# Running products in place of logarithm and exponential in a state-space scan with a cosine-gated FFN

## The chip, the cores and the metric

The kernel runs on one core of a Trainium2 chip. The metric is device time in microseconds (us). A kernel's time is the median of several runs; each run also records the length of its instruction span and the mean clock that the throttle granted to TensorE. TensorE does the matmuls (PE in the profile, PEld for its weight loads), DVE is VectorE, ACT is ScalarE, POOL is GpSimd, SP issues the DMAs.

## The reference, cut to what matters

For 4 batches, 8 heads and 768 positions, a decaying state of 16 x 32 is carried along the sequence; then an FFN with `h * cos(h)` follows.

```python
cum = np.cumsum(np.log(np.clip(a, 1e-06, 1.0)), axis=-1)         # in a chunk
L = np.exp(cum[..., :, None] - cum[..., None, :]) * causal       # decay from j to i
y = ((C @ B.T) * L) @ x + (C @ state) * np.exp(cum)[..., None]
state = np.exp(total) * state + sum_j(B_j x_j * exp(total - cum_j))
...
h = y @ w_in;  g = h * np.cos(h);  out = g @ w_out
```

The kernel works in six chunks of 128 positions. A decay between two positions is a product of `a`, so it can come from sums of logarithms or from a running product.

## The kernel before

One FFN **step** takes 128 of the 2048 inner columns for all four batches of a chunk: `first(n)` makes `h`, `gate(n-1)` the cosine and the product, `second(n-3)` the output sum. There are 96 steps, 16 a chunk. During the steps of chunk c the scan of chunk c+1 is done, one batch in three steps: decays and transposes (`turn`), then `intra`, then `finish` with the state update (`carry`). In the steps of chunk 0 the weights are also rounded, piece by piece: `grade` (ACT, POOL), then `join` (DVE twice, then an integer add on POOL).

```python
# the start: decays of whole chunks from sums of logarithms
ACT.activation(la, la, AF.Ln)
def whole():
    for u in range(NU):
        PE.transpose(lt_ps[:, u], la[:, u], ident[0:RB, 0:RB])
    ACT.copy(out=laT, in_=...)
    for i, tri in enumerate((upto, after, ones)):
        PE.matmul(d_ps, lhsT=tri, rhs=laT, start=True, stop=True)
        ACT.activation(dec[:, i], d_ps, AF.Exp)
    ACT.activation(..., quarter, AF.Sin)              # loads the sine's table
...
# in the loop
V.tensor_tensor_scan(out=l, data0=arow, data1=unit, initial=0.0, op0=mult, op1=add)   # lam
G.tensor_tensor(out=sc[:, i], in0=src, in1=dec[:, d, c] ..., op=ALU.mult)   # C and B scaled
PE.transpose(tp[:, 2], sc[:, 0, heads(b)] ..., ident)                       # scaled C
...
V.tensor_tensor(out=new, in0=s_ps, in1=own, op=ALU.mult)                    # carry
G.tensor_tensor(out=old, in0=state.pop((c - 1, b)), in1=dec[:, 2, c, ...], op=ALU.mult)
G.tensor_tensor(out=new, in0=new, in1=old, op=ALU.add)
...
for n in range(NC * NF + LAG):
    first(n)                                    # PE, then ACT k, DVE w
    if c == 0: grade(*order[n + 3])             # ACT mag and last, POOL clamp
    gate(n - 1)                                 # ACT sine, DVE gT
    second(n - LAG)
    if c == 0: join(*order[n + 2])              # DVE, DVE, POOL add
    # carry, then decays and turn, intra or finish of one batch of chunk c + 1
```

Of the kernel before, what the change touches and what calls it, by code (L numbers as in the profile page):

```python
# [8 lines left out]
FP32 = mybir.dt.float32  # L9
U32 = mybir.dt.uint32  # L10
I32 = mybir.dt.int32
AF = mybir.ActivationFunctionType
ALU = mybir.AluOpType
# [12 lines left out]
def kernel(  # L26
# [22 lines left out]
    nc = tc.nc  # L49
    V, ACT, G, PE = nc.vector, nc.scalar, nc.gpsimd, nc.tensor  # L50

    NB, H, S, D = x.shape
    N = B.shape[-1]
    P = 128
# [25 lines left out]
    def bank(shape, name, tag="scan"):  # L80
        return psum.tile(shape, FP32, tag=tag, bufs=BANKS[tag], name=name)


    raw, arow = {}, {}
    ones = const.tile([P, P], FP32, name="ones")
    V.memset(ones, 1.0)

    def fill(dst, times=1):

        for _ in range(times):  # L90
            PE.matmul(dst, lhsT=ones, rhs=ones.unsqueeze(1).to_broadcast([P, dst.shape[1], P]),  # L91
                      start=True, stop=True, skip_group_check=True)


    a_cut = dram.tile([NB, H, S], FP32, name="a_cut")

    def load(c, each=False):
# [13 lines left out]
    def load_a(c, seqs=range(NB)):  # L111
        if c >= NC:
            return
        for b in seqs:
            arow[c, b] = t = rows.tile([P, H, P], FP32, tag="arow", name="arow")
            nc.sync.dma_start(
                out=t, in_=a_cut[b, :, c * P:(c + 1) * P].unsqueeze(0).to_broadcast([P, H, P]))

    a_in = const.tile([RB, NU, P], FP32, name="a_in")
    nc.sync.dma_start(  # L120
# [60 lines left out]
    for n in range(6):  # L181
# [5 lines left out]
    quarter = const.tile([P, 1], FP32, name="quarter")  # L187
    V.memset(quarter, HALF_PI)

    upto = const.tile([P, P], FP32, name="upto")  # L190
    G.affine_select(out=upto, in_=ones, pattern=[[1, P]], compare_op=ALU.is_ge, fill=0.0,
                    base=0, channel_multiplier=-1)
    after = const.tile([P, P], FP32, name="after")
    G.affine_select(out=after, in_=ones, pattern=[[-1, P]], compare_op=ALU.is_gt, fill=0.0,
                    base=0, channel_multiplier=1)

    unit = const.tile([P, H, P], FP32, name="unit")
    V.tensor_copy(out=unit, in_=ident.unsqueeze(1).to_broadcast([P, H, P]))

# [8 lines left out]
    V.tensor_tensor(out=slot, in0=own[:, 0:HH, 0], in1=own[:, HH:H, 0], op=ALU.add)  # L208


    la = const.tile([RB, NU, P], FP32, name="la")
    V.tensor_scalar(out=la, in0=a_in, scalar1=1e-6, scalar2=1.0, op0=ALU.max, op1=ALU.min)
    cut = const.tile([RB, NU, P], FP32, name="cut")
    G.tensor_scalar(out=cut, in0=a_in, scalar1=1.0, scalar2=1e-6, op0=ALU.min, op1=ALU.max)
    G.memset(cut[:, :, 0:1], 0.0)
    nc.sync.dma_start(out=a_cut.rearrange("(u b) h (c p) -> (b h c) u p", u=NU, p=P), in_=cut)
    ACT.activation(la, la, AF.Ln)
    dec = const.tile([P, 3, NC, NB * H], FP32, name="dec")

    def whole():  # L220

        lt_ps = bank([P, NU, RB], "lt_ps")
        for u in range(NU):
            PE.transpose(lt_ps[:, u], la[:, u], ident[0:RB, 0:RB])
        laT = const.tile([P, NB * H * NC], FP32, name="laT")
        ACT.copy(out=laT, in_=lt_ps.rearrange("p u r -> p (u r)"))
        for i, tri in enumerate((upto, after, ones)):
            d_ps = bank([P, NB * H, NC], "d_ps")
            PE.matmul(d_ps.rearrange("p r c -> p (r c)"), lhsT=tri, rhs=laT,
                      start=True, stop=True)  # L230
            ACT.activation(dec[:, i].rearrange("p c r -> p r c"), d_ps, AF.Exp)

        ACT.activation(const.tile([P, 1], FP32, name="sine"), quarter, AF.Sin)


    scaled, lam, state, part, yT = {}, {}, {}, {}, {}

    def prep(c):

        if c >= NC:  # L240
            return
        bc = raw[c][0]
        scaled[c] = sc = scan.tile([P, 2, NB * H, N], FP32, tag="sc", name="sc")
        for i, (src, d) in enumerate(((bc[:, 1], 0), (bc[:, 0], 1))):
            if i == 0 and c == 0:
                continue
            G.tensor_tensor(
                out=sc[:, i], in0=src,
                in1=dec[:, d, c].unsqueeze(2).to_broadcast([P, NB * H, N]), op=ALU.mult)

    def heads(b):
        return slice(b * H, (b + 1) * H)
# [14 lines left out]

    def decays(c, b):

        lam[c, b] = l = scan.tile([P, H, P], FP32, tag="lam", bufs=3, name="lam")  # L270
        if c > 0:
            V.tensor_tensor_scan(  # L272
                out=l.rearrange("p h i -> p (h i)"),
                data0=arow.pop((c, b)).rearrange("p h i -> p (h i)"),
                data1=unit.rearrange("p h i -> p (h i)"), initial=0.0,
                op0=ALU.mult, op1=ALU.add)
            return
        for t, a_ps in enumerate(spread.pop(b)):
            V.tensor_tensor_scan(
                out=l[:, t * HH:(t + 1) * HH].rearrange("p h i -> p (h i)"),  # L280
                data0=a_ps.rearrange("p h i -> p (h i)"),
                data1=unit[:, 0:HH].rearrange("p h i -> p (h i)"), initial=0.0,
                op0=ALU.mult, op1=ALU.add)

    def turn(c, b):
        bc, sc = raw[c][0], scaled.get(c)
        tp = bank([P, 3, P], "tp")
        PE.transpose(tp[:, 0], bc[:, 0, heads(b)].rearrange("p h n -> p (h n)"), ident)
        PE.transpose(tp[:, 1], bc[:, 1, heads(b)].rearrange("p h n -> p (h n)"), ident)
        if c > 0:  # L290
            PE.transpose(tp[:, 2], sc[:, 0, heads(b)].rearrange("p h n -> p (h n)"), ident)  # L291

        cT = scan.tile([P, HH, P], FP32, tag="cT", name="cT")
        for t in range(HH):
            ACT.activation(cT[:, t], tp[:, 1], AF.Copy, scale=slot[:, t:t + 1])  # L295
        bcT = scan.tile([P, 2, P], FP32, tag="bcT", name="bcT")
        if c > 0:
            ACT.copy(out=bcT, in_=tp[:, 0:3:2])
        else:
            ACT.copy(out=bcT[:, 0], in_=tp[:, 0])  # L300
        part[c, b] = (bcT, cT)

    def intra(c, b):
# [36 lines left out]
    def carry(c, b):  # L340
        if c == NC - 1:
            return
        xr, sc = raw[c][1], scaled[c]
        s_ps = bank([P, H, D], "s_ps")
        PE.matmul(s_ps.rearrange("p h d -> p (h d)"),  # L345
                  lhsT=sc[:, 1, heads(b)].rearrange("p h n -> p (h n)"),
                  rhs=xr[:, b].rearrange("p h d -> p (h d)"), start=True, stop=True)
        state[c, b] = new = states.tile([P, H, D], FP32, tag="state", name="state")
        V.tensor_tensor(out=new, in0=s_ps, in1=own, op=ALU.mult)  # L349
        if c > 0:  # L350
            old = scan.tile([P, H, D], FP32, tag="old", name="old")
            G.tensor_tensor(
                out=old, in0=state.pop((c - 1, b)),
                in1=dec[:, 2, c, heads(b)].unsqueeze(2).to_broadcast([P, H, D]), op=ALU.mult)
            G.tensor_tensor(out=new, in0=new, in1=old, op=ALU.add)  # L355


    hp, turns, gT, o = {}, {}, {}, {}
# [39 lines left out]


    tags = (("h", "h"), ("h", "o"), ("h", "h"), ("h", "o"))  # L400
    fill(bank([P, 1, P], "warm", "o"), 8)
    spread_a(0, tags[0])
    whole()
    spread_a(1, tags[1])
    decays(0, 0)
    turn(0, 0)
    decays(0, 1)
    turn(0, 1)
    prep(0)
    intra(0, 0)  # L410
    spread_a(2, tags[2])
    decays(0, 2)
    intra(0, 1)
    finish(0, 0)
    spread_a(3, tags[3])
    decays(0, 3)
    turn(0, 2)
    turn(0, 3)
    finish(0, 1, 1)
    grade(*order[0])  # L420
    intra(0, 2)
    join(*order[0])
    intra(0, 3)
    finish(0, 2, 2)
    finish(0, 3, 2)
    grade(*order[1])
    grade(*order[2])
    join(*order[1])
    join(*order[2])
    load(1)  # L430
    for b in range(NB):
        load_a(1, (b,))
        for n in (6 + 2 * b, 7 + 2 * b):
            fetch(*order[n])
# [4 lines left out]
    for n in range(NC * NF + LAG):  # L439
        c, f = divmod(n, NF)  # L440
        if n < NC * NF:
            if f == 0 and c > 0:
                load(c + 2)
            first(n)
        if c == 0 and n + 3 < len(order):
            grade(*order[n + 3])
        if 0 <= n - 1 < NC * NF:
            gate(n - 1)
        if n >= LAG:
            second(n - LAG)  # L450
        if c == 0 and n + 2 < len(order):
            join(*order[n + 2])
        if n < NB:
            carry(0, n)
        if n == 1:
            prep(1)
        if c + 1 < NC:
            b, j = divmod(f - 3, 3)
            if 0 <= b < NB:
                if j == 0:  # L460
                    decays(c + 1, b)
                (turn, intra, finish)[j](c + 1, b)
            if f == NF - 1:
                raw.pop(c + 1)
                load_a(c + 2)
                prep(c + 2)


# [28 lines left out]
```

## Time and profile before

| | first trace | second trace, taken later |
|---|---|---|
| time of that run, us | 437.95 | 435.16 |
| span, us | 436.2 | 433.4 |
| mean granted clock | 0.992 | 0.996 |
| step 0 starts | 30.34 | 27.63 |
| step 6 starts | 55.33 | 52.53 |
| step 16 starts | 101.58 | 98.78 |
| step 16 to the end | 334.6 | 334.6 |

The median was 435.42 us. The second trace is of the usual kind. Here are its stretches of 2 us around the place where the first trace's clock was 0.50. Columns: stretch, length, busy time and count of PE, PEld, DVE, ACT and POOL, then granted clock, DMA share and GB/s.

```profile
12.00:14.00 2.00, 1.65 (x9) 0.90 (x10) 0.49 (x1) 1.49 (x7) 0.68 (x1) 1.00 1.02 324
14.00:16.00 2.00, 2.00 (x18) 1.57 (x16) 2.00 (x4) 0.00 (x0) 0.00 (x0) 1.00 1.05 392
```

The clock stays at 1.00. Nearly all that differs between the two traces lies before step 0 (from there to step 16 they take 71.2 us each). The times show the two kinds too: of the 48 runs of the kernel before that were taken for comparison, 36 lie between 434.85 and 435.65 us and 12 between 437.95 and 438.05 us, with nothing between.

### The profile page before, as it was taken

How to read it: one execution, taken by the hardware profiler on the slowest of the kernel's cores; microseconds unless marked ns; L12 is line 12 of the kernel's file. 1: busy time of each engine (PE TensorE's matmuls, PEld its weight loads, DVE VectorE, ACT ScalarE, POOL GpSimd, SP SyncE). 2: the span in 40 equal slices, each digit the busy share in tenths (PEclk: the TensorE clock that was granted, in tenths of full speed). 3: DMA queues.
4: the chain of work that ended last, by engine and by line, in shares of the span. 5: the costliest groups of instructions: out<-in, count | busy, mean ns of one | idle time of the engine just before them, and what ended most of it. 6: DMA issues, size and time to landing. Idle time of an engine off the chain costs nothing.

```text
span 436.2 us, 5099 instructions
## 1 busy us (share of the span) xinstructions
PE 424.1 (97%) x1918; PEld 274.8 (63%) x1918; DVE 241.6 (55%) x332; ACT 184.8 (42%) x383; POOL 72.5 (17%) x87
## 2 busy tenths in 40 slices
PE   8898999999999999999999999999999999999996
PEld 8544656656666656666566665666656666666665
DVE  4657976873654653546553465554465545344332
ACT  4366656543532433534442444433344433343332
POOL 2027664753011013010113001112000000000000
PEclk9898999999999999999999999999999999999999
DMA  7999698156211147111119021001010000010001
GB/s 92 315 131 345 213 136 139 48 80 66 67 31 48 50 71 75 50 48 48 50 32 114 27 70 50 29 20 50 0 50 0 0 2 0 2 48 0 0 2 48
DMA packets 103017, 28.84 MB, mean 66 GB/s; under 512 B 74960, under 2 KB 98896, under 8 KB 102992
## 3 DMA queue, kind: packets, MB, share of 16 engines
q1 hardware_dynamic: 102992, 28.51, 32.3%
q8 instruction: 15, 0.25, 0.2%
q14 instruction: 10, 0.08, 0.1%
HBM read 25.26 MB, written 3.24 MB: 65 GB/s over the span
## 4 chain that ended last, share of the span: by engine, by line
PE 91%; ACT 3%; POOL 2%; DVE 1%; issue 1%; ACTq 0%; POOLq 0%
PE hp L364 37%; PE o L385 36%; PE g L310 5%; PE y L331 3%; PE s_ps L345 2%; POOL w_in L176 2%; PE y L327 2%; PE a_ps L264 2%; PE warm L91 1%; ACT mag L156 1%; ACT cT L295 1%; DVE mag L172 1%; DVE mag L170 1%; ACT last L158 1%; PE y L91 0%
## 5 line engine op out<-in xcount | busy, mean ns | idle before, releaser
L364 PE MATMUL hp<-yT,w_in 128*128 128x512 f32 x384 | 184.6, 603 | 4.8 <-POOL w_in L176 4.2
L385 PEld LDWEIGHTS o<-w_out,gT 128*128 128x128 f32 x768 | 146.1, 190 | 59.3 <-issue 44.4
L385 PE MATMUL o<-w_out,gT 128*128 128x256 f32 x768 | 181.0, 379 | 0.0
L370 DVE SCALAR_TENSOR_TENSOR w<-hp,k 128x512 f32<-128x512 f32 x96 | 66.2, 690 | 135.1 <-ACT k L368 135.1
L368 ACT ACTIVATE k<-hp 128x512 int32<-128x512 f32 x96 | 57.3, 597 | 185.0 <-PE hp L364 184.6
L364 PEld LDWEIGHTS hp<-yT,w_in 128*128 128x128 f32 x384 | 69.8, 191 | 70.6 <-issue 48.5
L377 DVE TENSOR_TENSOR gT<-hp,w 128x512 f32<-128x512 f32 x96 | 66.3, 691 | 5.9 <-ACT w L375 5.7
L375 ACT ACTIVATE w<-w,quarter 128x512 f32<-128x512 f32 x96 | 68.5, 713 | 0.1
L272 DVE TENSOR_TENSOR_SCAN lam<-arow,unit 128x1024 f32<-128x1024 f32 x20 | 46.6, 2329 | 0.0
L355 POOL TENSOR_TENSOR state<-state,old 128x256 f32<-128x256 f32 x16 | 11.6, 725 | 185.2 <-DVE state L349 185.0
L313 DVE TENSOR_TENSOR m<-g,lam 128x512 f32<-128x512 f32 x48 | 30.9, 684 | 16.5 <-PE g L310 16.5
L295 ACT ACTIVATE cT<-tp,slot 128x128 f32<-128x128 f32 x96 | 27.4, 371 | 14.3 <-PE tp L291 12.4
L310 PE MATMUL g<-cT,bcT 64*128 64x512 f32 x96 | 28.5, 656 | 2.0 <-ACT bcT L300 1.9
L336 ACT COPY yT<-y 128x256 f32<-128x256 f32 x24 | 9.0, 376 | 35.5 <-PE y L331 35.5
L349 DVE TENSOR_TENSOR state<-s_ps,own 128x256 f32<-128x256 f32 x20 | 8.4, 422 | 18.6 <-PE s_ps L345 18.6
L176 POOL TENSOR_TENSOR w_in<-mag,last 128x512 uint32<-128x512 uint32 x8 | 14.0, 1751 | 12.8 <-DVE mag L172 12.8
L331 PE MATMUL y<-m,xr 128*32 128x128 f32 x384 | 15.5, 279 | 0.0
L159 POOL TENSOR_SCALAR mag<-mag 128x512 f32<-128x512 f32 x16 | 11.8, 738 | 16.1 <-ACT mag L156 16.1
L310 PEld LDWEIGHTS g<-cT,bcT 64*128 64x128 f32 x96 | 7.5, 185 | 10.5 <-ACT w L375 5.6
L345 PE MATMUL s_ps<-xr,sc 128*128 128x256 f32 x40 | 14.0, 434 | 0.0
L176 POOL TENSOR_TENSOR w_out<-mag,last 128x512 uint32<-128x512 uint32 x8 | 12.1, 1506 | 10.3 <-DVE mag L172 10.3
L327 PEld LDWEIGHTS y<-bcT,state 128*128 128x128 f32 x80 | 12.1, 191 | 1.0
(59 smaller groups left out, 190.4 us busy)
## 6 DMA issues: line engine op xcount, KB each, us to landing
arow<-a_cut SPq DMA_DIRECT2D x20, 512.0 KB, 4.0
words<-in_moe_w_in_dram SPq DMA_DIRECT2D x8, 512.0 KB, 6.5
words<-in_moe_w_out_dram SPq DMA_DIRECT2D x8, 512.0 KB, 7.0
out_dram<-ob SPq DMA_DIRECT2D x12, 256.0 KB, 2.2
xr<-in_x_dram SPq DMA_DIRECT2D x5, 512.0 KB, 8.8
bc<-in_B_dram SPq DMA_DIRECT2D x5, 256.0 KB, 7.3
bc<-in_C_dram SPq DMA_DIRECT2D x5, 256.0 KB, 9.4
xr<-in_x_dram SPq DMA_DIRECT2D x4, 128.0 KB, 3.7
```

The source lines that it names most:

```text
L176: G.tensor_tensor(out=dst.bitcast(U32), in0=bits.rearrange("p (k f) -> p k f", k=k), in1=last.rearrange("p (k f) -> p k f", k=k), op=ALU.add)
L272: V.tensor_tensor_scan(out=l.rearrange("p h i -> p (h i)"), data0=arow.pop((c, b)).rearrange("p h i -> p (h i)"), data1=unit.rearrange("p ...
L295: ACT.activation(cT[:, t], tp[:, 1], AF.Copy, scale=slot[:, t:t + 1])
L310: PE.matmul(g[u], lhsT=bcT[r, 0], rhs=cT[r], start=True, stop=True)
L313: V.tensor_tensor(out=m[:, hs], in0=g[u], in1=l[:, hs], op=ALU.mult)
L331: PE.matmul(y[32 * q:32 * q + 32, t], lhsT=xr[:, b, h], rhs=m[:, h], start=(c == 0 and t == 0), stop=True, tile_position=(0, 32 * q), skip ...
L364: PE.matmul(hp[n], lhsT=w_in[:, k, f * P:(f + 1) * P], rhs=yT[c][:, k], start=(k == 0), stop=(k == KT - 1))
L368: ACT.activation(k, hp[n], AF.Copy, bias=0.25, scale=INV_2PI)
L370: V.scalar_tensor_tensor(out=w, in0=hp[n], scalar=INV_2PI, in1=k, op0=ALU.mult, op1=ALU.subtract)
L375: ACT.activation(cos, cos, AF.Sin, bias=quarter, scale=TWO_PI)
L377: V.tensor_tensor(out=gT[n], in0=hp.pop(n), in1=cos, op=ALU.mult)
L385: PE.matmul(o[c][b // 2][:, b % 2], lhsT=g[:, b * P:(b + 1) * P], rhs=w_out[:, f], start=(f == 0 and b % 2 == 0), stop=(f == NF - 1), skip ...
```

## The change

Its intent: no logarithm, no exponential and no change of activation table; one transpose less per batch and chunk; the state update in one operation. The decay up to i becomes a second running product (`reach`) over rows of `a` that a DMA spreads over the partitions, and C is scaled as it is copied out of its transpose. B's decay is the last column of the scan that is there anyway.

```diff
-    ACT.activation(la, la, AF.Ln)
-    def whole(): ...                              # sums, Exp, tables
+    def load_along(c):                            # 4 new DMAs a chunk, 64 KB each
+        for b in range(NB):
+            nc.sync.dma_start(out=t[:, b], in_=a_all[b, :, c * P:(c + 1) * P] ...)
...
     (in decays)
+            V.tensor_tensor_scan(out=r, data0=along[c][:, b], data1=ones, initial=1.0,
+                                 op0=ALU.mult, op1=ALU.mult)               # reach
+        G.tensor_tensor(out=sc, in0=raw[c][0][:, 0, heads(b)],
+                        in1=lam[c, b][:, :, P - 1:P] ..., op=ALU.mult)      # B scaled
     (in turn)
-            PE.transpose(tp[:, 2], sc[:, 0, heads(b)] ..., ident)
+            V.tensor_tensor(out=bcT[:, 1], in0=tp[:, 1], in1=reach[c, b], op=ALU.mult)
     (in carry)
-            G.tensor_tensor(out=old, ...)
-            G.tensor_tensor(out=new, in0=new, in1=old, op=ALU.add)
+            V.scalar_tensor_tensor(out=new, in0=state.pop((c - 1, b)),
+                                   scalar=reach[c, b][:, P - 1:P], in1=new, op0=mult, op1=add)
     (the start)
-    fill(bank([P, 1, P], "warm", "o"), 8)
+    fill(bank([P, 1, P], "warm", "o"), 6)
     ...
+    grade(*order[1]); grade(*order[2])            # these moved ahead of finish(0, 3)
     finish(0, 3, 2)
+    join(*order[2]); join(*order[1])              # was 1, then 2
     load(1)
+    load_along(1)                                 # ahead of the weight pieces from 6 on
```

More of the change, by code (lines that the diff above doesn't have):

```diff
@@ L81, in bank @@
         return psum.tile(shape, FP32, tag=tag, bufs=BANKS[tag], name=name)
-    raw, arow = {}, {}
+    raw, arow, along = {}, {}, {}
     ones = const.tile([P, P], FP32, name="ones")
@@ L92, in fill @@
                       start=True, stop=True, skip_group_check=True)
+    a_all = dram.tile([NB, H, S], FP32, name="a_all")
     a_cut = dram.tile([NB, H, S], FP32, name="a_cut")
@@ L117, in load_a @@
                 out=t, in_=a_cut[b, :, c * P:(c + 1) * P].unsqueeze(0).to_broadcast([P, H, P]))
+    def load_along(c):
+        if c >= NC:
+            return
+        along[c] = t = rows.tile([P, NB, P], FP32, tag="along", bufs=2, name="along")
+        for b in range(NB):
+            nc.sync.dma_start(
+                out=t[:, b], in_=a_all[b, :, c * P:(c + 1) * P].unsqueeze(1)
+                .to_broadcast([H, N, P]))
     a_in = const.tile([RB, NU, P], FP32, name="a_in")
@@ L188 @@
     V.memset(quarter, HALF_PI)
-    upto = const.tile([P, P], FP32, name="upto")
-    G.affine_select(out=upto, in_=ones, pattern=[[1, P]], compare_op=ALU.is_ge, fill=0.0,
-                    base=0, channel_multiplier=-1)
-    after = const.tile([P, P], FP32, name="after")
-    G.affine_select(out=after, in_=ones, pattern=[[-1, P]], compare_op=ALU.is_gt, fill=0.0,
-                    base=0, channel_multiplier=1)
     unit = const.tile([P, H, P], FP32, name="unit")
@@ L208 @@
     V.tensor_tensor(out=slot, in0=own[:, 0:HH, 0], in1=own[:, HH:H, 0], op=ALU.add)
-    la = const.tile([RB, NU, P], FP32, name="la")
-    V.tensor_scalar(out=la, in0=a_in, scalar1=1e-6, scalar2=1.0, op0=ALU.max, op1=ALU.min)
     cut = const.tile([RB, NU, P], FP32, name="cut")
@@ L215 @@
     G.memset(cut[:, :, 0:1], 0.0)
-    nc.sync.dma_start(out=a_cut.rearrange("(u b) h (c p) -> (b h c) u p", u=NU, p=P), in_=cut)
-    ACT.activation(la, la, AF.Ln)
-    dec = const.tile([P, 3, NC, NB * H], FP32, name="dec")
-    def whole():
-        lt_ps = bank([P, NU, RB], "lt_ps")
-        for u in range(NU):
-            PE.transpose(lt_ps[:, u], la[:, u], ident[0:RB, 0:RB])
-        laT = const.tile([P, NB * H * NC], FP32, name="laT")
-        ACT.copy(out=laT, in_=lt_ps.rearrange("p u r -> p (u r)"))
-        for i, tri in enumerate((upto, after, ones)):
-            d_ps = bank([P, NB * H, NC], "d_ps")
-            PE.matmul(d_ps.rearrange("p r c -> p (r c)"), lhsT=tri, rhs=laT,
-                      start=True, stop=True)
-            ACT.activation(dec[:, i].rearrange("p c r -> p r c"), d_ps, AF.Exp)
-        ACT.activation(const.tile([P, 1], FP32, name="sine"), quarter, AF.Sin)
-    scaled, lam, state, part, yT = {}, {}, {}, {}, {}
-    def prep(c):
-        if c >= NC:
-            return
-        bc = raw[c][0]
-        scaled[c] = sc = scan.tile([P, 2, NB * H, N], FP32, tag="sc", name="sc")
-        for i, (src, d) in enumerate(((bc[:, 1], 0), (bc[:, 0], 1))):
-            if i == 0 and c == 0:
-                continue
-            G.tensor_tensor(
-                out=sc[:, i], in0=src,
-                in1=dec[:, d, c].unsqueeze(2).to_broadcast([P, NB * H, N]), op=ALU.mult)
+    la = const.tile([RB, NU, P], FP32, name="la")
+    V.tensor_scalar(out=la, in0=a_in, scalar1=1.0, scalar2=1e-6, op0=ALU.min, op1=ALU.max)
+    for dst, src in ((a_cut, cut), (a_all, la)):
+        nc.sync.dma_start(out=dst.rearrange("(u b) h (c p) -> (b h c) u p", u=NU, p=P), in_=src)
+    ACT.activation(const.tile([P, 1], FP32, name="sine"), quarter, AF.Sin)
+    scaled, lam, reach, state, part, yT = {}, {}, {}, {}, {}, {}
     def heads(b):
@@ L276, in decays @@
                 op0=ALU.mult, op1=ALU.add)
+            reach[c, b] = r = scan.tile([P, P], FP32, tag="reach", bufs=2, name="reach")
+            V.tensor_tensor_scan(out=r, data0=along[c][:, b], data1=ones, initial=1.0,
+                                 op0=ALU.mult, op1=ALU.mult)
+            decay_b(c, b)
             return
@@ L283, in decays, with decay_b @@
                 op0=ALU.mult, op1=ALU.add)
+        decay_b(c, b)
+    def decay_b(c, b):
+        if c == NC - 1:
+            return
+        scaled[c, b] = sc = scan.tile([P, H, N], FP32, tag="sc", bufs=NB, name="sc")
+        G.tensor_tensor(out=sc, in0=raw[c][0][:, 0, heads(b)],
+                        in1=lam[c, b][:, :, P - 1:P].to_broadcast([P, H, N]), op=ALU.mult)
     def turn(c, b):
-        bc, sc = raw[c][0], scaled.get(c)
-        tp = bank([P, 3, P], "tp")
+        bc = raw[c][0]
+        tp = bank([P, 2, P], "tp")
         PE.transpose(tp[:, 0], bc[:, 0, heads(b)].rearrange("p h n -> p (h n)"), ident)
         PE.transpose(tp[:, 1], bc[:, 1, heads(b)].rearrange("p h n -> p (h n)"), ident)
-        if c > 0:
-            PE.transpose(tp[:, 2], sc[:, 0, heads(b)].rearrange("p h n -> p (h n)"), ident)
         cT = scan.tile([P, HH, P], FP32, tag="cT", name="cT")
@@ L296, in turn @@
         bcT = scan.tile([P, 2, P], FP32, tag="bcT", name="bcT")
+        ACT.copy(out=bcT[:, 0], in_=tp[:, 0])
         if c > 0:
-            ACT.copy(out=bcT, in_=tp[:, 0:3:2])
-        else:
-            ACT.copy(out=bcT[:, 0], in_=tp[:, 0])
+            V.tensor_tensor(out=bcT[:, 1], in0=tp[:, 1], in1=reach[c, b], op=ALU.mult)
         part[c, b] = (bcT, cT)
@@ L342, in carry @@
             return
-        xr, sc = raw[c][1], scaled[c]
+        xr, sc = raw[c][1], scaled.pop((c, b))
         s_ps = bank([P, H, D], "s_ps")
-        PE.matmul(s_ps.rearrange("p h d -> p (h d)"),
-                  lhsT=sc[:, 1, heads(b)].rearrange("p h n -> p (h n)"),
+        PE.matmul(s_ps.rearrange("p h d -> p (h d)"), lhsT=sc.rearrange("p h n -> p (h n)"),
                   rhs=xr[:, b].rearrange("p h d -> p (h d)"), start=True, stop=True)
@@ L350, in carry @@
         if c > 0:
-            old = scan.tile([P, H, D], FP32, tag="old", name="old")
-            G.tensor_tensor(
-                out=old, in0=state.pop((c - 1, b)),
-                in1=dec[:, 2, c, heads(b)].unsqueeze(2).to_broadcast([P, H, D]), op=ALU.mult)
-            G.tensor_tensor(out=new, in0=new, in1=old, op=ALU.add)
+            V.scalar_tensor_tensor(out=new, in0=state.pop((c - 1, b)),
+                                   scalar=reach[c, b][:, P - 1:P], in1=new,
+                                   op0=ALU.mult, op1=ALU.add)
     hp, turns, gT, o = {}, {}, {}, {}
@@ L400 @@
     tags = (("h", "h"), ("h", "o"), ("h", "h"), ("h", "o"))
-    fill(bank([P, 1, P], "warm", "o"), 8)
+    fill(bank([P, 1, P], "warm", "o"), 6)
     spread_a(0, tags[0])
-    whole()
-    spread_a(1, tags[1])
     decays(0, 0)
     turn(0, 0)
+    spread_a(1, tags[1])
     decays(0, 1)
     turn(0, 1)
-    prep(0)
     intra(0, 0)
@@ L415 @@
     spread_a(3, tags[3])
+    turn(0, 2)
     decays(0, 3)
-    turn(0, 2)
     turn(0, 3)
     finish(0, 1, 1)
+    intra(0, 2)
     grade(*order[0])
-    intra(0, 2)
     join(*order[0])
@@ L424 @@
     finish(0, 2, 2)
-    finish(0, 3, 2)
     grade(*order[1])
     grade(*order[2])
+    finish(0, 3, 2)
+    join(*order[2])
     join(*order[1])
-    join(*order[2])
     load(1)
+    load_along(1)
     for b in range(NB):
@@ L454 @@
             carry(0, n)
-        if n == 1:
-            prep(1)
         if c + 1 < NC:
@@ L465 @@
                 load_a(c + 2)
-                prep(c + 2)
+                load_along(c + 2)
 _INS = ['x', 'a', 'B', 'C', 'moe_w_in', 'moe_w_out']
```

## The prediction

> **What bounds the kernel now.** I began with the page: busy shares, then the 40 slices, then the chain that ended last.
>
> ```profile
> PE 424.1 (97%) x1918; PEld 274.8 (63%) x1918; DVE 241.6 (55%) x332; ACT 184.8 (42%) x383; POOL 72.5 (17%) x87
> ...
> PE   8898999999999999999999999999999999999996
> ...
> PEclk9898999999999999999999999999999999999999
> DMA  7999698156211147111119021001010000010001
> ...
> PE hp L364 37%; PE o L385 36%; PE g L310 5%; PE y L331 3%; PE s_ps L345 2%; POOL w_in L176 2%; PE y L327 2%; PE a_ps L264 2%; PE warm L91 1%; ACT mag L156 1%; ACT cT L295 1%; DVE mag L172 1%; DVE mag L170 1%; ACT last L158 1%; PE y L91 0%
> ```
>
> TensorE is busy 97% of the span and is 91% of the chain. The digits of the PE row below 9, the clock digits of 8 and nearly all DMA work lie in the first four slices (11 us each). So there are two regimes: a start of some 45 us, where other engines and waits count, and a steady part where only TensorE instructions count. The chain in order of time shows the steady part:
>
> ```profile
> 113.79 1.73 PE o L385 x8
> 115.52 0.11 PE tp L288
> 115.63 0.11 PE tp L289
> 115.74 0.11 PE tp L291
> 115.85 1.72 PE hp L364 x4
> ```
>
> No gap: each piece starts where the last ended. An FFN step costs 1.72 + 1.73 = 3.45 us, and a transpose 0.11 us in this queue (its own duration, 0.27 us, overlaps its neighbours). One scan unit (a chunk and a batch) adds 3.2 us per three steps: 115.85 to 129.41 is 13.56, less 3 x 3.45. In the same stretch DVE's big scan ends 0.28 us before the next thing it is asked for can start, and gT comes most of a step before TensorE wants its bank. DVE's small additions there are hidden.
>
> The start, from the same chain and the timeline:
>
> ```profile
> 8.29 1.26 PE d_ps L229 x6
> 9.55 1.17 ACT dec L231 x3
> 10.72 1.28 ACT L233
> ...
> 12.22 1.03 ACT cT L295 x4
> 13.25 0.16 ACT bcT L300
> ...
> 13.46 1.81 PE g L310 x4
> ```
>
> This is the reader's main line: logarithm, transposed sums, three exponentials and two changes of the activation table stand in line ahead of the first chunk's C and B, because ScalarE works in order. In the table of 2 us stretches TensorE is busy only 0.55 us of 12-14, and its clock is 0.50 in 14-16 and 0.70 in 16-18. The first FFN matmul starts at 30.34. The list of waits then gives what holds TensorE later:
>
> ```profile
> PE hp L364 <- POOL w_in L176: 4.2, 4, 2.0
> PEld hp L364 <- POOL w_in L176: 6.5, 4, 2.4
> POOL state L355 <- DVE state L349: 185.0, 13, 24.0
> ```
>
> Four FFN steps (2, 4, 8 and 14) wait for a rounded weight slice, whose chain is ACT, POOL, DVE, POOL. The 185 us of the last line are idleness of an engine nobody waits for. At two of the four, the last link is slow:
>
> ```profile
> 61.36 2.28 DVE L272 TENSOR_TENSOR_SCAN lam<-arow,unit 128x1024 f32<-128x1024 f32 x1
> 61.53 3.17 POOL L176 TENSOR_TENSOR w_in<-mag,last 128x512 uint32<-128x512 uint32 x1 [1.85 <-DVE mag L172]
> ```
>
> **What the Trainium skill says.** "GPSIMD Engine Reference", section 1, says the SBUF interface is shared with VectorE and that DVE instructions with two SBUF inputs contend. The trace agrees: this add takes 1.27 us alone and 3.17 when it meets the scan. "ScalarE: Activation LUTs", "What ACT_TABLE_LOAD costs", gives 1283 ns for a load; the trace has three of exactly 1283 ns. It adds a drain of 1380 ns, which I do not see: the exponential starts as the load ends (9.55). "TensorE: Matmul & The Clock Gate", Part 1, puts an idle array at half clock; the 0.50 after the hole at 12-14 agrees, as does 0.50 in 38-40 after TensorE was busy only 1.15 of 2 us.
>
> **The change, part by part.**
> 1. TensorE, steady part. The transpose of scaled C goes: 20 x 0.11 = 2.2 us. Two of these sit just ahead of the waits at steps 8 and 14 and one in the filling of the pipeline, where TensorE waits anyway: 17 x 0.11 = 1.9 us gained.
> 2. Start. Removed: two transposes and six matmul records of the sums (7.45 to 9.4 on TensorE, about 1.7 us), ACT's logarithm, copy, three exponentials and two of three table loads (8.26 to 12.22, 4 us in ACT's queue), two POOL masks (1.0 us, not on the path, since POOL then waits for a memset) and four of 16 warm-up records. I re-laid the start with the trace's own durations. First spread at 4.2 instead of 4.5 (it then waits for the clipped decays, ready at 4.13); B and C of batch 0 landed at about 4.9; transposes at 7.2 (11.05 before); cT and bcT done at 9.0 (13.4); first g at 9.7 (13.46). DVE then becomes the limit: eight scans of 1.17, eight products of 0.65 and one join of 1.1 make 15.7 us; before they took from 6.65 to 28.53, and I get 6.3 to 24.1 with the holes that remain. Two weight slices are now graded before the last yT copy (four ACT pieces at 0.58 = 2.3 us), so first(0) starts at about 26.3 instead of 30.34: **4.0 us gained**.
> 3. Filling, steps 0 to 6. Before, from 30.34 to 55.49, 25.2 us against some 20 without waits. The joined second slice used to come at 36.8; with the new order at about 28.3, before step 2 wants it, so that wait (1.97 us) and the half clock after it go, as does POOL's 2.1 us of scaling at 40.3. But then DVE (w, gT, joins, states, first scan) is in line, and words number 6 land at 35.7 now, perhaps at 37.5 with the new transfers; ACT, in order, must wait for them at step 3. I get step 6 at about 49 instead of 55.5, that is **2.4 us gained** beyond the 4.0.
> 4. DVE's additions. A row scan costs 2280/1024 = 2.2 ns an element, so 128 elements about 0.35 us (20 times, 7 us); C times reach from PSUM, 128 wide, about 0.25 us (5 us); the state's one operation on 128x256, about 0.4 us as the 0.42 of L349 (16 times, 6.5 us). 19 us in all; DVE goes from 242 to about 258 less what it no longer waits inside instructions, under 62%. In the steady part it is hidden. Where DVE holds the shared interface at steps 6 and 12, a second scan right after the first can hold the weight add 0.35 us longer: up to 0.7 us lost, I count 0.4.
> 5. POOL: 16 x (0.62 + 0.73) and eleven scalings of 1.06 go, twenty smaller ones come. Nobody waits for these: 0 in the steady part.
> 6. DMA: a second 96 KB write and 64 KB reads. In 14 to 50 us the DMA share is at its top, so this costs 1 to 2 us of arrival time, counted in 3; later the share is 0.3 and it is hidden.
>
> Sum: -4.0 - 2.4 - 1.9 + 0.4 = -7.9 us, so **427.5 us**, 1.8% less.
>
> **Rivals.**
> (a) *Weights by DMA set the end of the start.* Words 6 and 8 land at 35.7 and 40.2 and are used at 43.3 and 52.7, so there is slack of 7 us and more now; but I want to use 6 to 7 of it. If the added small-row transfers push words back by 3 us or more, part 3 is lost: some 430 to 431.
> (b) *DVE becomes the bound in steps 0 to 16.* It is busy 15.7 of 20 us in 40-60 already, and parts 4's 0.35 + 0.25 + 0.4 per three steps lift that to over 85%. For it: in the joins DVE stands in the weight chain itself. Against: joins and old waits overlap. It would turn 1 or 2 more steps into waits of about 1 us: 429 to 430.
> (c) *The start is shortened more than I think,* if TensorE never drops to half clock: the hole at 12-14 cost about 0.7 us in g and 1 us in the spread after it, and steps 2 and 3 cost 1.7 us more than later steps. Then 424.
> (d) *All the start's gain is absorbed* by the waits at steps 8 and 14. Against: their slices are graded and joined in step with the FFN itself (step n+2), with DMA long landed, so they move with it.
>
> **Range and chances.** Part 1 is nearly sure (1.5 to 2.2). Parts 2 and 3 together may be 3 to 9. That gives 424.3 to 431.2 for 8 in 10. The 2% line is at about 426.8, 0.7 below my centre, so: faster by over 2% 0.40, within 2% 0.59, slower 0.01.
>
> **What would show it.** First(0) near 26.3; step 6 near 49; only one table load on ACT; no clock of 0.5 after about 5 us; the steady three-step period 13.45 instead of 13.56; waits at steps 8 and 14 still there, with POOL's add near 3.2 to 3.5. I am wrong if step 0 moves by less than 2 us, if TensorE waits for DVE in the steady part, or if ACT sits in front of words 6 for over 3 us.

## The result, and the profile after

The changed kernel took 432.25 us in the median (432.02 to 432.90, 4 runs) against 435.44 us. A ratio here is the mean time of one kernel's fast runs over that of the other's fast runs of the same rounds, so it is not quite the ratio of the medians: 0.9929, with a 95% interval of 0.9912 to 0.9946. That is some 0.7% faster, "the same" at the 2% line, and above the predicted range of 424.3 to 431.2.

Three lines of the page of the changed kernel: busy shares, the clock in 40 slices, and the engines in the chain that ended last.

```profile
PE 419.0 (97%) x1886; PEld 270.4 (63%) x1886; DVE 263.6 (61%) x388; ACT 178.3 (41%) x376; POOL 46.2 (11%) x62
...
PEclk9999999999999999999999999999999999999999
...
PE 81%; DVE 6%; SPq 5%; DMA 2%; ACT 2%; issue 2%; POOL 1%; ACTq 0%; DVEq 0%
```

TensorE is still busy 97%, but DVE (6%) and the SP queue with its DMAs (5% and 2%) now stand in the chain, where TensorE had 91% before. DVE's share is a first sign that the start has a new limit. SP and DMA are not a sure one: the second trace of this kernel, taken later, has DVE at 6% again and neither of them in its chain. The next lines are the first matmuls of steps 0 and 6, first from the second trace of before, then from the trace of the changed kernel (its line numbers differ: L349 is L364 of before).

```profile
27.63 1.96 PE L364 MATMUL hp<-yT,w_in 128*128 128x512 f32 x4 [0.58 <-ACT yT L336]
...
52.53 1.88 PE L364 MATMUL hp<-yT,w_in 128*128 128x512 f32 x4
```

```profile
27.40 1.96 PE L349 MATMUL hp<-yT,w_in 128*128 128x512 f32 x4 [1.46 <-ACT yT L324]
...
50.56 1.88 PE L349 MATMUL hp<-yT,w_in 128*128 128x512 f32 x4
```

Against a usual run of before, step 0 starts 0.2 us earlier and step 6 2.0 us earlier. Step 16 starts at 97.70 (98.78 before), so in steps 6 to 16 some 0.9 us is given back. From step 16 to the end it takes 332.9 us in place of 334.6, 1.7 less, just the 16 transposes of 0.107 us in that part. The sum is 2.0 - 0.9 + 1.7 = 2.8 us, and the spans say 433.4 - 430.6 = 2.8.

So the steady part went as intended, and the question is the first 100 us: two tables of ACT and 4 us of its queue went, and TensorE gained 1.1 us from it.

### The profile page after: what moved, and what is told of

Its sections match the earlier page's. It is cut to its first block, busy times and chain, and to the rows that moved or that the text cites. A ratio compares the mean times of both kernels' runs of the same rounds, so it can differ in the third digit from the quotient of the medians.

```text
span 430.6 us, 5067 instructions
## 1 busy us (share of the span) xinstructions
PE 419.0 (97%) x1886; PEld 270.4 (63%) x1886; DVE 263.6 (61%) x388; ACT 178.3 (41%) x376; POOL 46.2 (11%) x62
## 4 chain that ended last, share of the span: by engine, by line
PE 81%; DVE 6%; SPq 5%; DMA 2%; ACT 2%; issue 2%; POOL 1%; ACTq 0%; DVEq 0%
PE hp L349 35%; PE o L370 34%; SPq L109 4%; PE g L298 4%; PE y L319 3%; PE s_ps L333 2%; PE y L315 2%; POOL w_in L187 1%; DVE mag L183 1%; DVE lam L250 1%; DMA words<-in_moe_w_out_dram 1%; DVE mag L181 1%; SPq L126 1%; DMA along<-a_all 1%; DVE gT L362 1%
## 5 line engine op out<-in xcount | busy, mean ns | idle before, releaser
L349 PE MATMUL hp<-yT,w_in 128*128 128x512 f32 x384 | 183.3, 600 | 5.2 <-POOL w_in L187 3.2
L349 PEld LDWEIGHTS hp<-yT,w_in 128*128 128x128 f32 x384 | 69.3, 190 | 70.7 <-issue 48.2
L284 ACT ACTIVATE cT<-tp,slot 128x128 f32<-128x128 f32 x96 | 27.4, 371 | 20.5 <-PE tp L280 20.5
L273 POOL TENSOR_TENSOR sc<-bc,lam 128x128 f32<-128x128 f32 x20 | 8.6, 430 | 208.1 <-DVE lam L250 117.4
L319 PEld LDWEIGHTS y<-m,xr 128*32 128x32 f32 x384 | 8.9, 109 | 5.9 <-DVE m L301 2.0
```

The source lines that it names most:

```text
L284: ACT.activation(cT[:, t], tp[:, 1], AF.Copy, scale=slot[:, t:t + 1])
L319: PE.matmul(y[32 * q:32 * q + 32, t], lhsT=xr[:, b, h], rhs=m[:, h], start=(c == 0 and t == 0), stop=True, tile_position=(0, 32 * q), skip ...
L349: PE.matmul(hp[n], lhsT=w_in[:, k, f * P:(f + 1) * P], rhs=yT[c][:, k], start=(k == 0), stop=(k == KT - 1))
```

## The experiments

Fifteen runs, told by question. "Changed" is the kernel of the diff. Each was traced once and timed in five rounds against the kernel before.

### Is the first trace of before a usual one?

The kernel before, without an edit.

> The kernel before, unchanged, for a second trace. The first trace has a span of 436.2 us and a clock of 0.992 in a run of 437.95 us, 2.5 us above its timed runs. Theory A (the first trace fell on a run with more half-clock stretches than the timed ones, and my prediction counted on getting those back): this trace and the timed runs show a clock of 0.996 or more and spans of 433.3 to 434.3, and step 2's first matmuls take about 2 us, not 3.0. Rival (the half clock belongs to every run of this kernel, and the profile only adds a constant): clock 0.992 and a span near 436 again. Ratio of times 1.000 in both.

Measured: 435.14 us, five runs at 434.95 to 435.16 with spans near 433.4, and one at 437.96 with a span of 436.2 and a clock of 0.992. Theory A holds: the first trace was of the rarer kind. One half of its expectation did not: the half clock after step 2 is there in the usual run as well (0.50 in 36 to 38 us, and the matmuls of step 2 take 2.62 us). The usual run starts step 0 2.7 us earlier, and that comes from two things. Its TensorE reaches its full rate sooner (the spacing of the small matmuls falls from 0.21 to 0.11 us at 4.7 us, in the first trace at 7.0), so the same 16 spreading matmuls, the first work after the warming ones, take 1.1 us less, as these lines show, first trace first:

```profile
4.70 3.02 PE L264 MATMUL a_ps<-cut,ident 96*128 96x128 f32 x16
```

```profile
4.67 1.95 PE L264 MATMUL a_ps<-cut,ident 96*128 96x128 f32 x16
```

The other 1.6 us are the half clock at 14 to 18 us, which the usual run lacks, although TensorE's hole ahead of it is the same 1.69 us in both.

### Where do the 0.9 us of steps 6 to 16 go?

The trace of the changed kernel shows DVE and POOL meeting. Columns: start, duration, engine, line.

```profile
52.24 1.26 DVE L338 SCALAR_TENSOR_TENSOR state<-state,reach 128x256 f32<-128x256 f32 x1
...
56.60 2.28 DVE L250 TENSOR_TENSOR_SCAN lam<-arow,unit 128x1024 f32<-128x1024 f32 x1
56.76 3.17 POOL L187 TENSOR_TENSOR w_in<-mag,last 128x512 uint32<-128x512 uint32 x1 [2.36 <-DVE mag L183]
...
58.80 1.42 DVE L256 TENSOR_TENSOR_SCAN reach<-along,ones 128x128 f32<-128x128 f32 x1
...
114.05 0.40 DVE L256 TENSOR_TENSOR_SCAN reach<-along,ones 128x128 f32<-128x128 f32 x1
...
122.15 0.49 DVE L338 SCALAR_TENSOR_TENSOR state<-state,reach 128x256 f32<-128x256 f32 x1
```

The last two lines are from chunk 1, where POOL adds no weights: the short scan takes 0.40 us and the update 0.49. In chunk 0 the same take 1.42 and 1.26: POOL's add waits for the long scan (3.17 in place of 1.27), and then the short scan waits for the add. Three experiments ask what that costs.

**State update back on POOL.** Edit in `carry`:

```diff
-            V.scalar_tensor_tensor(out=new, in0=old_state, scalar=reach[:, P - 1:P], in1=new, ...)
+            G.tensor_tensor(out=old, in0=old_state, in1=reach[:, P - 1:P] broadcast, op=mult)
+            G.tensor_tensor(out=new, in0=new, in1=old, op=add)
```

> The changed kernel with only the state update put back on POOL in two operations. Theory B (in chunk 0 DVE has become the limit, because its added two-input operations meet POOL's weight adds and are held: the one-operation update took 1.26 us there): 0.5 to 1.3 us faster than the changed kernel (432.3), nearly all before step 16. Rival C (the loss lies in the first 30 us, in the start and the DMA): within 0.3 us of it.

Measured: 433.03 us (432.40 to 433.56), no gain. Steps 6 to 16 take 47.10 us against 47.14. Theory B in this form falls: in the changed kernel's trace DVE still waits 0.83 us for ACT's sine two operations after the update of 1.26 us, so the update's collision costs nothing by itself.

**Short scan first.** The two scans in `decays` change places.

> The changed kernel with the short scan (reach) ahead of the long one (lam). Theory B2 (at steps 6 and 12 the long scan holds the shared interface as POOL's weight add starts, and TensorE waits 1.1 us each for that add at steps 8 and 14): the add now waits only for the short scan, takes about 1.6 us in place of 3.17, both waits go, and the kernel is 1.5 to 2.2 us faster than the changed one. Rival (DVE's total is what counts: the long scan then waits for the add instead): within 0.4 us.

Measured: 430.47 us (429.54 to 430.95). As expected the add takes 1.32 us and the step it feeds is no longer held (its TensorE wait of 1.1 us is gone), but the long scan is then held by the add (3.30 us), and the next product `m`, and TensorE behind it, come later: steps 6 to 16 take 46.21 us, 0.9 less than changed, not the 1.5 to 2.2 of the theory. The rest of its gain in time is not from this: its trace starts step 0 at 25.21, and that is the next question.

**Both moved to where DVE idles.** Between `w` and `gT` DVE waits some 0.8 to 1.0 us for ACT's sine, and POOL adds nothing then.

```diff
             first(n)
+        add_state()                     # the update that carry left for the next step
+        if (f - 3) % 3 == 0: reach_b(c + 1, (f - 3) // 3)
         grade(...); gate(n - 1)
```

> The changed kernel with the short scan and the one-operation state update both moved to where DVE waits for ACT's sine (between w and gT of a step), away from POOL's weight adds. Theory B (collisions on the interface, 1.0 us a unit for the scan and 0.9 for the update, are what made chunk 0 hardly shorter): steps 0 to 16 take 68.5 to 69.5 us in place of 70.3, 0.8 to 1.8 us faster; short scan about 0.4 us and update about 0.4 to 0.6 us there. Rival (DVE's load, not the collisions): under 0.4 us.

Measured: 429.74 us (429.15 to 430.76). The short scans take 0.43 us on average instead of 0.55, the updates 0.56 instead of 0.63. Steps 6 to 16 take 46.14 us, 1.0 less than in the changed kernel, and about what they take in before (46.25). So the loss of 0.9 us in this stretch is that of the collisions on DVE's line in chunk 0, and as the update alone cost nothing and the scans' order alone (e3) gave 0.9 us back, it is the short scan's. It can be avoided. The waits of 1.1 us for the weight adds at steps 8 and 14 stay in this version (1.0 in before).

### When does the start end, and who notices?

The traces of e3 and of the next run start step 0 at 25.21 and 24.49 us, though their first 20 us hold the same work as the changed kernel's, which starts it at 27.40.

**The new loads later.** Edit:

```diff
     load(1)
-    load_along(1)
     for b in range(NB):
         load_a(1, (b,)); fetch two weight pieces
+        if b == 0: load_along(1)
```

> The changed kernel with the four new row loads of chunk 1 issued after the first pair of weight pieces instead of ahead of them. Theory D (the new loads push the weight words back and ACT waits for them in order): 0.5 to 1.5 us faster, step 6 earlier by as much. Rival (words are there in time either way, DVE is the limit in steps 2 to 5): within 0.3 us.

Measured: three runs at 429.9 to 430.2 and three at 432.2 to 432.6, median 431.20. A split like that asked for another look at the changed kernel, and for a cause.

**The changed kernel again.**

> The changed kernel, unchanged, for more runs and a second trace. So far the same start took until 27.4 us (first trace of it, first FFN matmul) or 24.5 us (in another variant), depending on when TensorE reached full clock (10.8 or 4.4 us). Theory E (that moment is a matter of the run, not of the code): times of this kernel spread over 2 to 3 us, some runs near 430, others near 432.3. Rival (this code always warms late): all within 432.0 to 432.9, first FFN matmul at 27.4 again.

Measured: 432.61 to 434.34 us, step 0 at 27.59 in its trace: the rival's late start, with a wider spread than the rival said.

**Eight warming matmuls.** `fill(..., 6)` back to 8.

> The changed kernel with 8 warming matmuls in place of 6, as before had. Six end at 4.05 us, 0.07 us before the clipped decays are ready for the next group; eight leave no hole. Theory F (that hole is what delays the full clock[...] in part of the runs): all runs early, first FFN matmul at 24.5 to 25.5, median near 430.2 and a spread under 1 us. Rival E (the phase is random): same spread as the changed kernel's, and no gain in the median beyond 0.5 us.

Measured: 431.25 to 433.71, median 432.99. Its trace, of the fastest of its runs, starts early (step 0 at 25.12) and has step 6 at 49.43, but its times as a whole are hardly better than the changed kernel's (433.32 in the same rounds). The times that theory F expected did not come; why an early start can help this kernel so little is shown below.

**All together:** eight warming matmuls, DVE's moves, the loads later.

> Eight warming matmuls, the moves of the run above, and the row loads of chunk 1 after the first weight pieces, together. If theories B and F hold: 428.5 to 429.5 us, below both kernels. If neither: 430.5 to 432.

Measured: 428.82 us (428.13 to 429.27), ratio to before 0.9836 (0.9809 to 0.9862). That is the expected figure, in part by luck: it rested on theory F, which the run above had not borne out, and named no gain for the later loads. This beats both kernels. It is the base of the next runs, each of which takes one part out.

**The loads ahead again,** the rest as combined.

> The combined kernel with the row loads of chunk 1 back ahead of the first weight pieces. Theory D (with an early start, ACT stands in order before weight piece 6, which these loads push back): step 5 to 6 takes 6.3 us or more in place of 5.3, 0.7 to 1.3 us slower than the combined kernel. Rival: within 0.3 us.

Measured: 429.70 us (429.39 to 430.14), 0.9 slower; steps 5 to 6 take 6.65 us in place of 5.26. Theory D holds.

**Six warming matmuls,** the rest as combined.

> The combined kernel with six warming matmuls again. Theory F (fewer of them makes the full clock come late in many runs): some or all runs 1 to 2.5 us slower, spread over 2 us. Rival (the count does not matter, the phase of the clock gate does): first FFN matmul 0.6 us earlier where the clock comes early, median within 0.7 us of the combined kernel's on either side.

Measured: 428.53 us, five runs at 428.34 to 428.56 and one at 430.50. The count does not matter in the median.

**Place in the job, and a fuller window.** The kernel of the run above, now first of the kernels run together; the changed kernel with `fill(..., 12)`; the changed kernel without an edit, now last of them.

> The combined kernel with six warming matmuls, as run before (428.5), now first in the job, where the changed kernel stood in its late runs. If the place in the job decides: full clock near 10.8 us, 430.5 or more in all runs. If the code or chance decides: most runs at 428.3 to 428.9 as before.

> The changed kernel with 12 warming matmuls, which keep TensorE on full-array work until about 6.3 us if cold, at the cost of 1 to 2 us in the earliest start. Theory I (a window of the clock gate filled with the 96-row spreading matmuls and the short hole before them is not counted as busy): no run reaches full clock later than 8 us, times within 1 us of each other and no more than 431.5. Rival (chance, or something else in the code): spread of 2 us and more, some runs above 432.5.

> The changed kernel a third time, now last in the job. If the place in the job decides: full clock at 4.4 to 6 us and most runs near 430. If the code decides: 432.0 to 434 in all runs again and full clock near 10.8.

Measured: 428.78 us (four at 428.25 to 428.80, two at 430.6 and 430.9), 431.93 us (431.30 to 432.01) and 433.40 us (431.41 to 433.67). The place in the job decides nothing. Twelve warming matmuls give times within 0.7 us of each other, as theory I expected, but at 431.9 slightly above its bound of 431.5. The third run was the telling one, because its trace is of an early start. First, early and late side by side: the first spreading matmuls and the first transpose, in the first trace of the changed kernel and in this one.

```profile
4.12 3.78 PE L241 MATMUL a_ps<-cut,ident 96*128 96x128 f32 x16
7.70 0.42 PE L279 MATMUL tp<-ident,bc 128*128 128x128 f32 x1
```

```profile
4.14 2.15 PE L241 MATMUL a_ps<-cut,ident 96*128 96x128 f32 x16
6.13 0.27 PE L279 MATMUL tp<-ident,bc 128*128 128x128 f32 x1
```

The same 16 matmuls take 3.78 or 2.15 us, and a transpose 0.42 or 0.27: in the late start TensorE runs at its cold rate until about 10.3 us (there the spacing of its small matmuls falls from 0.21 to 0.11 us; the expectations say 10.8), in the early one until about 4.5. The code is the same. The early run then starts step 0 at 24.61, 2.8 us sooner. And yet it took 433.18 us. These lines of its trace say why.

```profile
37.28 0.67 ACT L167 ACTIVATE mag<-words 128x512 f32<-128x512 f32 x1 [2.71 <-DMA words<-in_moe_w_in_dram]
39.17 0.69 DVE L362 TENSOR_TENSOR gT<-hp,w 128x512 f32<-128x512 f32 x1 [2.40 <-ACT w L360]
47.72 1.28 DVE L301 TENSOR_TENSOR m<-g,lam 128x512 f32<-128x512 f32 x2
48.45 0.43 PE L319 MATMUL y<-m,xr 128*32 128x128 f32 x8 [1.94 <-DVE m L301]
...
50.65 2.64 PE L349 MATMUL hp<-yT,w_in 128*128 128x512 f32 x4
```

Read it from the top. At step 3 ACT, which works in order, is ready for weight piece 6 and idles 2.71 us until its DMA has landed at 37.3. The sine of step 2 stands behind that, so DVE's `gT` is 2.40 us late. DVE never makes this up: its joins, the scan and `m` are one line of work up to 49 us. TensorE waits 1.94 us for `m`, and after the hole the throttle grants half clock (0.50 in 50 to 52 us), so step 6 takes 2.64 us. It starts at 50.65, where the late start had it at 50.56. The whole head start of 2.8 us is gone. Not every early start loses so much: with eight warming matmuls (e6) the hole was 1.34 us, no half clock followed, and step 6 started at 49.43. The loss seems common: of the 16 runs of the changed kernel, the ten with a mean clock of 0.995 or 0.996 took 432.90 to 434.34 us, the six with 0.999 or more 431.41 to 432.61. That the ten had this hole is argued from their clock; one of them was traced.

The DMA queue shows what fixes that landing: first this run, then the run with the loads later (start and duration of each issue).

```profile
26.44 4.98 SPq L126 DMA_DIRECT2D along<-a_all  x4
...
31.97 0.58 SPq L153 DMA_DIRECT2D words<-in_moe_w_in_dram  x1
```

```profile
29.88 0.86 SPq L153 DMA_DIRECT2D words<-in_moe_w_in_dram  x1
...
31.29 2.83 SPq L126 DMA_DIRECT2D along<-a_all  x4
```

The four new loads hold the queue 5 us while the earlier loads still drain, and piece 6 is issued at 31.97 instead of 29.88. With them later (e4), ACT reads it at 35.5 and waits 1.05 us. With DVE's moves as well, step 6 starts at 47.68 after an early start (e11) and at 50.07 after a late one (e13): now 2.4 of 3.0 us come through, and the times of those two runs differ by as much, 428.56 against 430.86.

### What were the sums of logarithms worth?

The combined kernel with `whole()`, its masks, logarithm and table loads put back ahead of the first `turn`, unused.

> The combined kernel (428.8) with the removed sums of logarithms put back at the start, unused: masks, logarithm, two transposes, three triangular products, three exponentials, two more table loads. Theory G (that work stands in ACT's and TensorE's queues ahead of the first chunk and its removal reaches the end): first FFN matmul 2 to 3 us later and 1.5 to 3 us slower. Rival (the start is limited by DVE and by DMA, and the removal is absorbed): under 0.7 us slower.

Measured: 432.32 us (431.64 to 433.07), 3.5 us slower. Step 0 starts at 28.40 instead of 25.38 and step 6 at 50.97 instead of 47.95: 3.0 us, all of which reaches the end. Theory G holds, in a kernel whose DMA order and DVE line let it through.

### Was it the order of the last instructions of the start?

The kernel before, with only the changed kernel's order of `grade`, `join`, `intra` and `finish` at the end of the start.

> The kernel before with nothing but the changed kernel's order of the last instructions of the start (two weight pieces graded before the last yT copy, the second joined first). Theory H (the filling's gain of 2.4 us between steps 0 and 5 is a matter of this order, not of the new arithmetic): steps 0 to 5 take 17.3 to 18 us in place of 19.7, no half-clock stretch at 34 to 38, 1.5 to 2.5 us faster than before. Rival (POOL's removed scaling or the removed waits of the start made it): under 0.7 us.

Measured: 437.60 us (one run at 434.93, five at 437.5 to 438.0), no gain. Theory H falls, and its trace shows a wait moved:

```profile
38.74 2.26 POOL L247 TENSOR_TENSOR sc<-bc,dec 128x512 f32<-128x512 f32 x2
...
41.99 1.26 POOL L176 TENSOR_TENSOR w_in<-mag,last 128x512 uint32<-128x512 uint32 x1
...
43.31 3.65 PE L364 MATMUL hp<-yT,w_in 128*128 128x512 f32 x4 [2.41 <-POOL w_in L176]
```

TensorE no longer waits at step 2, but now 2.41 us at step 4, because POOL scales B and C ahead of that step's weight add, and after the hole the clock is halved. In the changed kernel the scaling is gone and the same wait is 0.99 us. So the order alone does not make the gain of 2.4 us between steps 0 and 5 (17.3 us in place of 19.7). The new arithmetic with the old order was not run; that both had to change together is argued from this wait.

## Why the prediction was wrong, point by point

**The base of the sum failed first.** "I re-laid the start with the trace's own durations", and took the difference, 7.9 us, from the median of the timed runs. But the trace was of a run 2.5 us above that median, with a later full clock and the half clock at 14 to 18 us that the removed hole was to cure. The prediction's "first(0) starts at about 26.3 instead of 30.34" compared with the rarer kind; the usual run starts it at 27.63. So 2.7 of the predicted 4.0 us were not there for the median. By the prediction's own sign ("I am wrong if step 0 moves by less than 2 us") this is the first failure: against the usual run it moved by 0.2 us. The rarer kind did gain 5.6 us of span (436.2 to 430.6), and none of the 16 runs of the changed kernel is at 438.

**Part 2, the start itself,** was right in kind. Like compared with like it gained 3 us: from 27.63 to 24.61 between an early start of before and one of the changed kernel, from 30.34 to 27.40 between the later ones (full rate at 7.0 and 10.3 us); and the sums put back cost the combined kernel 3.5 us. What was not foreseen is the late full clock: with the same code, step 0 then starts at 27.4 to 27.6, 1.1 us or more after the 26.3.

**Part 3, the filling, is the step that failed in size.** "I get step 6 at about 49" gave the steps 0 to 6 22.7 us (49 less 26.3). Measured: 23.2 after the late start of 27.40 and 26.0 after the early one of 24.61, so both reach step 6 at 50.6. After the early start the mechanism was the one named ("ACT, in order, must wait for them at step 3", words 6 "perhaps at 37.5"; measured 37.3), as was its effect in rival (a), but the landing does not move with the start, and DVE's chain from there to `m`, with the hole and the half clock after it, took 3.3 us more than I gave it. Of the branches named, rival (a), 430 to 431, comes nearest there, without its condition of words 3 us late: some 1.6 us (37.3 against the 35.7 of the first trace, within the 1 to 2 of part 6) were enough. After the late start ACT does not wait for words 6 (0.2 us in the second trace); there it is DVE's line alone that makes TensorE wait for `m`, and steps 5 to 6 take 5.85 us in place of 5.19.

**Part 4:** DVE's additions were hidden in the steady part, as predicted. In chunk 0 they cost 0.9 us in place of the counted 0.4. The place was right (the short scan behind the long one, at the weight adds), and the size was not: held by POOL's add, the scan takes 1.42 us, not the 0.35 that I allowed for. Rival (b) was half of this story.

**Part 1** was right: 16 transposes after step 16, 1.7 us, and the steady period is 13.45 us (before 13.56). **Part 5** as to the state update was right, nobody waits for it; as to the scaling it was right inside part 3, since its removal made room for the weight add. Rival (d) was wrong: the waits at steps 8 and 14 moved with the rest and absorbed nothing.

Of the misses in the profiled run, the base is 2.7, the late full clock in part 2 is 1.1, part 3 is 0.7 (1.7 of the 2.4 us came, against the usual run) and part 4 with the swallowed transposes 0.7 us; together 5.2, where the span fell by 2.8 in place of 7.9. The median time missed by 4.75 us.

**What stays open:** what decides whether TensorE reaches its full rate at 4.1 to 7.0 us, as in 13 of the 17 traces, or only at 10.3 to 10.7, as in four. The place in the job was tried and does not decide it; runs with the same first 20 us differ. The number of warming matmuls is not cleared: all four late traces are among the nine of kernels with six, and none of the eight traces with eight or twelve is late. The change itself went from eight to six, so it may have brought its own late starts. The medians of six and eight are alike (428.53 and 428.82 in the combined kernel), but three of the twelve runs with six there and in its repeat took 430.5 us or more, and none of the five with eight. That it is a matter of a clock window's phase was only argued.

## What to carry to other kernels

Before a difference worked out on a trace is taken from a median, compare that trace's own run and clock with the timed runs; a trace 2.5 us above the median holds 2.5 us that the median cannot gain. When a start is shortened, ask which arrivals stay at their fixed time: here a weight piece landing at 37.3 us, in front of an in-order engine, turned 2.8 us of head start into one wait. And when work is moved to an engine, look for a moment in which it idles and its neighbour on the same interface is quiet: the same scan cost 0.40 or 1.42 us by its place alone.

## What the Trainium skill lacked or had wrong

- "TensorE: Matmul & The Clock Gate", the table of why this matters, asks for no idle gaps above about 3 us. Here half clock followed holes of 1.94 us (clock 0.50 at 50 to 52 us) and of 2.41 us (step 4 of the order-only run took 3.65 us). After one of 1.69 us, ahead of the first chunk's `g`, it followed in the first trace of before and not in the second.
- The same page, Part 1, has full clock after one busy window of about 3.4 us. In the changed kernel TensorE was busy from 1.12 us on, but for 0.07 us, until it reached its full rate, which was at 4.5 us in one trace and at 10.3 and 10.7 in two others.
- "ScalarE: Activation LUTs", on table loads, adds a drain of 1380 ns to the 1283 ns of a load. The runs show the load and no drain: in the run with the sums put back the load ran from 7.07 to 8.35 us and the exponential began at 8.36.
